# RWKV-7 attention with a hard-swish FFN on one core: FFN pieces moved ahead beside the second inversion, earlier K~ and B~, a denser third inversion

## Chip, cores and metric

One core of one Trainium2 chip. The metric is the device time of a whole execution in microseconds. Before and after are read from one profiled execution each, and the times from several executions of both on the same chip.

## The reference, cut to what matters

Two blocks follow each other. The attention runs a recurrence over 768 steps for 4 x 8 heads with a 40 x 40 state; its output, 3072 tokens of 320 features, goes through an FFN of width 2048.

```python
for t in range(S):
    y[:, :, t] = np.einsum('bhd,bhde->bhe', rt, state)
    Sa = np.einsum('bhde,bhe->bhd', state, at)
    state_decay = state * wt[:, :, None, :] - np.einsum('bhd,bhe->bhde', Sa, bt)
    state = state_decay + np.einsum('bhd,bhe->bhde', vt, kt)
...
h = x @ w_in
g = h * np.clip(h + 3.0, 0.0, 6.0) / 6.0
out = g @ w_out
```

## The kernel before

The sequence is cut into 24 units of work (`NK`; i below counts them from 0), four to a group (`NU`). A unit is prepared ahead of time (stages W, gam, A, B, K, F, factor, E, EV) and then stepped through (RT, R, C, S, U, UT, rS, sn, H, y, move). Each group needs one triangular inversion: a chain of about 60 short VectorE instructions that ends in the transposes tb (L552) and tt. RR (L625) is the product R plus EV, and S a turned copy of the state; U, UT and rS need them. The FFN of finished units is cut into pieces, nine for each half unit, that are handed out between attention stages to keep TensorE busy. `pieces(n)` hands out n pieces, `aside(n)` n steps of the inversion. The engines run their instructions in the order in which these calls are made, and that order is all the change touches.

One half unit of FFN (five pieces of expand, four of contract; each line with `yield` ends a piece):

```python
for c in range(2):
    for t in range(2):
        for i in range(NQ):
            nc.tensor.matmul(out=hp[c][:, i, :], lhsT=win[...], rhs=xt[:, t, :], ...)     # L806
        yield True
for i in range(NQ): ...
        nc.tensor.matmul(out=hp[c][:, i, :], lhsT=win2[...], rhs=xt[half(c), 2, :], ...)  # L811
for c in range(2):
    nc.scalar.activation(out=gt[:], in_=hp[c][:], func=AF.Relu, bias=three[:], scale=1.0) # L816
    nc.vector.scalar_tensor_tensor(out=gt[:], in0=gt[:], scalar=6.0, in1=hp[c][:], ...)   # L817
yield True
# contract, one half unit later:
            nc.tensor.matmul(out=op[:], lhsT=gts[c][:, n, :], rhs=wout[...], ...)         # L830
```

The inversion, and the product that needs its tb (L572):

```python
def invert(F, third):
    nc.vector.transpose(out=fb...)                                   # L531
    nc.gpsimd.affine_select(out=x...)                                # L534
    ...
    for i in range(1, L - 1):
        nc.vector.tensor_tensor(out=pv, ...)                         # L543
        yield
        nc.vector.tensor_tensor(out=rest, in0=rest, in1=pv, ...)     # L549
        yield
    nc.vector.transpose(out=tb..., in_=x[:])                         # L552
    yield
    nc.vector.transpose(out=tt..., ...)                              # L556
    ...

def third_block(F, tb, tt, n):
    ...
            nc.tensor.matmul(out=zp[x]..., lhsT=F..., rhs=tb..., ...)        # L572
```

The stages that a block can be given, and the loop over blocks (m counts blocks, four to a unit). A block issues all its products, then all their evictions (the copies out of PSUM), and takes its PSUM banks from five; when they don't suffice, `together` evicts in between:

```python
AHEAD_STAGES = [["W", "gam"], ["A", "B"], ["F", "K"], ["E", "factor"], ["EV"]]
...
for i in range(NU, NK):
    for j in range(BLOCKS):
        rate, inversion = 3.5, 0
        if i + AHEAD >= NK + NU - 1:
            rate = 4.5
        if i == NU and j == 0:
            inversion = 3
        a_block(m)
        if side and i > NU or i % NU == NU - 1 and rate < 4:
            rate, inversion = 6.2, 2
        if i % NU < 2 and j < 2:
            feed(rate / 2, inversion)
            if i % NU == 0:
                aside(3 * L)          # the rest of the inversion
            block(i, j)               # L572, L584
            rate /= 2
        feed(rate, inversion)         # piece, steps, piece, steps, ...
        m += 1
```

`factor` makes K~ and B~ (L473) out of the loaded K and B, and then issues the loads of the next unit's B and K into the same buffers.

Of the kernel before, what the change touches and what calls it, by code (L numbers as in the profile page):

```python
# [29 lines left out]
def kernel(  # L30
# [43 lines left out]
    B, H, T, D = r.shape  # L74
# [3 lines left out]
    NU = 2 * NP  # L78
# [447 lines left out]
    def invert(F, third):  # L526



        fb = inv.tile([P, L, L], F32, name="fb")  # L530
        nc.vector.transpose(out=fb[:].rearrange("p t s -> p s t"),  # L531
                            in_=F[:, :, 0:L].rearrange("p h s -> p s h"))
        x = inv.tile([P, L, L], F32, name="x", tag="x", bufs=1)
        nc.gpsimd.affine_select(out=x[:], in_=fb[:], pattern=[[1, L], [-1, L]],  # L534
                                compare_op=ALU.is_gt, fill=0.0, base=0, channel_multiplier=0)
        nc.gpsimd.memset(_ap(x[:], 0, [[L + 1, L]]), 1.0)
        for _ in range(3):
            yield
        prod = inv.tile([P, NH, L], F32, name="prod", tag="tt")
        for i in range(1, L - 1):  # L540
            n = L - 1 - i
            pv = _ap(prod[:], 0, [[i, n], [1, i]])
            nc.vector.tensor_tensor(  # L543
                out=pv, in0=_ap(x[:], (i + 1) * L + i, [[L, n], [0, i]]),
                in1=_ap(x[:], i * L, [[0, n], [1, i]]), op=ALU.mult,
            )
            yield
            rest = x[:, i + 1:L, 0:i]
            nc.vector.tensor_tensor(out=rest, in0=rest, in1=pv, op=ALU.add)  # L549
            yield  # L550
        tb = inv.tile([P, NH, L], F32, name="tb", tag="fb")
        nc.vector.transpose(out=tb[:].rearrange("p h t -> p t h"), in_=x[:])  # L552
        yield

        tt = inv.tile([P, NH, L], F32, name="tt", tag="tt")
        nc.vector.transpose(out=tt[:].rearrange("p h j -> p j h"),  # L556
                            in_=x[:].rearrange("p r j -> p j r"))
        third.append((F, tb, tt))
        for z in range(0, P, BL):
            yield  # L560
            nc.scalar.activation(out=tinv[z:z + L, :, 0:L], in_=tb[z:z + L], func=AF.Copy)
            nc.gpsimd.tensor_copy(tinv[z + L:z + BL, :, L:BL], tb[z + L:z + BL])
        yield
# [299 lines left out]
    def pieces(n):  # L863

        owed[0] += n
        while owed[0] >= 1:
            owed[0] -= 1
            if not next(stream):
                owed[0] = 0.0

    def aside(n, weight=0):

        for _ in range(n):
            if side and next(side[0], side) is side:
                side.popleft()
            for _ in range(weight):
                next(weights, None)
# [10 lines left out]
    third, F, group_F = [], None, []  # L888

    def prepared(i):  # L890
        nonlocal F
        if i >= NK:
            return None
        if i % NU == 0:
            F = inv.tile([P, NH, BL], F32, name="F", tag="F", bufs=2)
            group_F.append(F)
        return prepare(i, F)
# [39 lines left out]
    def block(i, j):  # L937

        if i % NU < 2:
            if j == 0:  # L940
                n = i % NU
                blocks[i] = third_block(*third[-1], 2 * n)
            run(blocks[i])
# [31 lines left out]
        pass  # L975
    for _ in range(16):
        aside(2)
        pieces(0.75)



    OWN_STAGES = [["RT", "VT"], ["R", "C", "S"], ["U", "UT", "rS"], ["sn", "H"], ["y"],
                  ["move", "move2"]]
    AHEAD_STAGES = [["W", "gam"], ["A", "B"], ["F", "K"], ["E", "factor"], ["EV"]]


    PRODUCTS = ["RT", "VT", "W", "S", "A", "B", "K", "factor",
# [5 lines left out]
    BLOCKS = 4  # L993

    def together(stages):

        begun, banks = [], 0

        def finish():
            begun.sort(key=lambda x: RESULTS.index(x[0]))  # L1000
            for _, rest in begun:
                for _ in rest:
                    pass
            begun.clear()
            shared[0] = None

        for name in PRODUCTS:
            for stage in stages.get(name, []):
                if name in TURNS:
                    need = 1  # L1010
                else:
                    width = WIDTH.get(name, NPR * BL)
                    need = 2 * (shared[0] is None or shared[1] + width > 512)
                if banks + need > 5:
                    finish()
                    banks, need = 0, 1 if name in TURNS else 2
                banks += need
                rest = stage()
                next(rest)
                begun.append((name, rest))  # L1020
        begun.extend((name, stage()) for name in stages if name not in PRODUCTS
                     for stage in stages[name])
        finish()

    begins = {u: max(3 * (u - 2 * NU), BLOCKS * (u - NU - AHEAD)) for u in range(2 * NU, NK)}
    coming, ahead, own = deque(range(2 * NU, NK)), {}, {}

    def a_block(m):

        if coming and begins[coming[0]] == m:  # L1030
            u = coming.popleft()
            ahead[u, m] = prepared(u), AHEAD_STAGES
        if m % BLOCKS == 0 and m // BLOCKS + NU < NK:
            i = m // BLOCKS + NU
            own[i, m] = step(i), OWN_STAGES
        stages = {}
        for (u, begin), (fs, order) in sorted(own.items()) + sorted(ahead.items()):
            if m - begin < len(order):
                for name in order[m - begin]:
                    stages.setdefault(name, []).append(fs[name])  # L1040
        together(stages)
        if any(u % NU == NU - 1 and m - begin == 2 for u, begin in ahead):
            third.clear()
            side.append(invert(group_F[-1], third))

    def feed(n, inversion):

        whole = int(n)
        for k in range(whole):
            pieces(1)  # L1050
            aside(inversion)
        pieces(n - whole)

    m = 0
    for i in range(NU, NK):
        for j in range(BLOCKS):
            rate, inversion = 3.5, 0
            if i + AHEAD >= NK + NU - 1:
                rate = 4.5
            if i == NU and j == 0:  # L1060
                inversion = 3
            a_block(m)
            if side and i > NU or i % NU == NU - 1 and rate < 4:
                rate, inversion = 6.2, 2
            if i % NU < 2 and j < 2:
                feed(rate / 2, inversion)
                if i % NU == 0:
                    aside(3 * L)
                block(i, j)
                rate /= 2  # L1070
            feed(rate, inversion)
            m += 1
    for _ in range(2):
        a_block(m)
        m += 1
# [32 lines left out]
```

## Time and profile before

| | before |
|---|---|
| time, median | 892.05 us (888.48 to 892.34, 4 runs) |
| span of the profiled execution | 891.7 us |
| TensorE busy | 791.5 us, 89% |
| TensorE idle from 195 to 406 us | 211 - 188.1 = 22.9 us |
| TensorE idle from 406 us to the end | 485.75 - 479.4 = 6.3 us, of it 4.3 behind its last product |

The last two rows tell where a change of order can gain: TensorE is full from the tenth unit (i = 9, at 406 us) on, so what counts is how early that point comes.

### The profile page before, as it was taken

The page shows a single profiled execution, that of the slowest core. Times are in us where ns is not written, and L with a number is a line of the kernel's source. Part 1 is how long each engine was busy: PE and PEld are TensorE (multiplying, and loading weights), DVE is VectorE, ACT ScalarE, POOL GpSimd, SP SyncE. Part 2 cuts the span into 40 slices and gives each one's busy share as a digit, 9 for nine tenths or more (in the row PEclk, how much of TensorE's full clock was granted, in tenths as well). Part 3 has the DMA queues.
Part 4 walks back from the last instruction along what each step waited for, and adds up shares of the span by engine and source line. Part 5 has one row for each costly group of instructions (what it writes and reads, how often), then busy time and mean ns, then how long its engine had stood idle before and what let it go on. Part 6 is the DMA issues. An engine that isn't in the chain of part 4 may idle for free.

```text
span 891.7 us, 36217 instructions
## 1 busy us (share of the span) xinstructions
PE 791.5 (89%) x16128; PEld 673.8 (76%) x16128; DVE 533.8 (60%) x1141; ACT 289.2 (32%) x694; POOL 152.1 (17%) x295
## 2 busy tenths in 40 slices
PE   4611878898698999899999999999999999999998
PEld 3511766777587787688888888888888888888886
DVE  7998777968744457835469744579544775122211
ACT  1334644232333222233323433322434233322211
POOL 4321010220121120211211311220222102000000
PEclk8755678998798899989999999999999999999999
DMA  6543333431122222203221222321232111010000
GB/s 131 89 113 93 111 107 93 73 69 20 34 41 56 36 45 47 46 20 63 52 41 37 47 48 42 58 43 36 49 56 42 25 26 23 17 25 17 19 18 15
DMA packets 175979, 45.08 MB, mean 51 GB/s; under 512 B 157904, under 2 KB 173264, under 8 KB 175824
## 3 DMA queue, kind: packets, MB, share of 16 engines
q1 hardware_dynamic: 174768, 42.61, 23.7%
q8 instruction: 127, 2.08, 1.0%
q10 hardware_dynamic: 1056, 0.16, 0.1%
q14 instruction: 28, 0.23, 0.1%
HBM read 34.08 MB, written 3.93 MB: 43 GB/s over the span
## 4 chain that ended last, share of the span: by engine, by line
PE 59%; issue 1%; DVE 1%; POOL 0%; DMA 0%; ACT 0%; SPq 0%
PE o L830 19%; PE h L806 16%; PE h L811 5%; PE any L358 4%; PE any L376 3%; PE any L708 2%; PE any L731 2%; PE any L653 1%; PE any L450 1%; PE any L572 1%; PE any L619 1%; PE any L584 1%; PE any L674 1%; PE any L690 1%; PE any L638 1%
## 5 line engine op out<-in xcount | busy, mean ns | idle before, releaser
L830 PE MATMUL o<-wout,gt 128*128 128x320 f32 x768 | 238.0, 455 | 0.2 <-DVE gt L817 0.2
L806 PE MATMUL h<-xt,win 128*128 128x128 f32 x1536 | 198.0, 283 | 0.6 <-issue 0.5
L806 PEld LDWEIGHTS h<-xt,win 128*128 128x128 f32 x1536 | 187.1, 196 | 10.5 <-issue 1.3
L830 PEld LDWEIGHTS o<-wout,gt 128*128 128x128 f32 x768 | 141.9, 194 | 56.8 <-issue 3.9
L817 DVE SCALAR_TENSOR_TENSOR gt<-gt,h 128x512 f32<-128x512 f32 x96 | 61.3, 680 | 93.2 <-ACT gt L816 93.2
L816 ACT ACTIVATE gt<-h,three 128x512 f32<-128x512 f32 x96 | 60.8, 686 | 136.1 <-PE h L811 136.1
L741 POOL TENSOR_TENSOR yg<-ys,gam 128x512 f32<-128x512 f32 x24 | 40.4, 1685 | 240.4 <-DVE ys L738 133.8
L543 DVE TENSOR_TENSOR prod<-x 128x30 f32<-128x30 f32 (+9 forms) x180 | 63.3, 352 | 11.7 <-POOL x L534 6.7
L549 DVE TENSOR_TENSOR x<-x,prod 128x30 f32<-128x30 f32 (+9 forms) x180 | 61.9, 344 | 4.4
L473 POOL TENSOR_TENSOR KBt<-K,rgt 128x320 f32<-128x320 f32 x24 | 23.9, 996 | 232.4 <-ACT rgt L465 214.0
L811 PE MATMUL h<-xt,win 64*128 64x128 f32 x768 | 55.8, 285 | 0.0
L385 DVE COPY_PREDICATED score<-mask,any 128x256 f32<-128x256 int32 x143 | 53.0, 431 | 0.0
L572 PE MATMUL any<-tb,F 32*32 32x32 f32 x768 | 16.6, 203 | 38.7 <-DVE tb L552 38.7
L715 DVE TENSOR_TENSOR state<-any,state 128x160 f32<-128x160 f32 x48 | 13.3, 316 | 62.9 <-PE any L376 58.4
L811 PEld LDWEIGHTS h<-xt,win 64*128 64x128 f32 x768 | 46.6, 187 | 5.1 <-issue 0.2
L412 DVE RECIPROCAL gam<-prods 128x256 f32<-128x256 f32 x24 | 41.4, 1738 | 14.1 <-POOL yg L741 14.0
L738 DVE TENSOR_TENSOR ys<-any,ys 128x256 f32<-128x256 f32 x48 | 18.1, 418 | 52.6 <-PE any L500 27.2
L572 PEld LDWEIGHTS any<-tb,F 32*32 32x32 f32 x768 | 15.3, 119 | 41.8 <-issue 40.9
L401 DVE TENSOR_TENSOR_SCAN prods<-wm,start 128x528 f32<-128x528 f32 x24 | 30.1, 1253 | 21.4 <-ACT wm L398 19.7
L427 DVE RECIPROCAL rgam<-prods 128x256 f32<-128x256 f32 x24 | 41.7, 1739 | 0.0
L625 DVE TENSOR_TENSOR RR<-any,EV 128x160 f32<-128x160 f32 x48 | 13.3, 317 | 43.6 <-PE any L376 38.5
L267 ACT ACTIVATE parts<-parts,low 128x256 uint32<-128x256 uint32 x40 | 20.3, 508 | 57.3 <-DVE parts L265 57.1
(136 smaller groups left out, 1177.5 us busy)
## 6 DMA issues: line engine op xcount, KB each, us to landing
raw<-in_moe_w_out_dram SPq DMA_DIRECT2D x20, 256.0 KB
B<-in_b_dram SPq DMA_DIRECT2D x48, 80.0 KB
K<-in_k_dram SPq DMA_DIRECT2D x48, 80.0 KB
V<-in_v_dram SPq DMA_DIRECT2D x96, 40.0 KB
R<-in_r_dram SPq DMA_DIRECT2D x96, 40.0 KB
out_dram<-ob SPq DMA_DIRECT2D x48, 80.0 KB
W<-in_w_dram SPq DMA_DIRECT2D x40, 80.0 KB
A<-in_a_dram SPq DMA_DIRECT2D x40, 80.0 KB
```

The lines of the kernel that those rows point to most:

```text
L385: nc.vector.copy_predicated(out=x[:, 4 * i:4 * i + 4, :], mask=mask4, data=o[i])
L412: nc.vector.reciprocal(gv[:, :, 0:HB], o["prods"][:, :, 0, 1:HB + 1][:, :, ::-1])
L427: nc.vector.reciprocal(rv[:, :, HB:BL], o["prods"][:, :, 1, 1:HB + 1])
L543: nc.vector.tensor_tensor(out=pv, in0=_ap(x[:], (i + 1) * L + i, [[L, n], [0, i]]), in1=_ap(x[:], i * L, [[0, n], [1, i]]), op=ALU.mult,)
L549: nc.vector.tensor_tensor(out=rest, in0=rest, in1=pv, op=ALU.add)
L572: nc.tensor.matmul(out=zp[x][z:z + L, h, :], lhsT=F[z + L:z + BL, n * H + h, L:BL], rhs=tb[z + L:z + BL, n * H + h, :], start=True, stop=True,
L741: nc.gpsimd.tensor_tensor(out=yg[:], in0=m["ys"][:].rearrange("p r q t -> p r (q t)"), in1=o["G"][:], op=ALU.mult)
L806: nc.tensor.matmul(out=hp[c][:, i, :], lhsT=win[:, t, j * P:(j + 1) * P], rhs=xt[:, t, :], start=(t == 0 and i == 0), stop=False)
L811: nc.tensor.matmul(out=hp[c][:, i, :], lhsT=win2[half(c), (j0 + i) * P:(j0 + i + 1) * P], rhs=xt[half(c), 2, :], start=False, stop=(i == N ...
L816: nc.scalar.activation(out=gt[:], in_=hp[c][:], func=AF.Relu, bias=three[:], scale=1.0)
L817: nc.vector.scalar_tensor_tensor(out=gt[:], in0=gt[:], scalar=6.0, in1=hp[c][:], op0=ALU.min, op1=ALU.mult)
L830: nc.tensor.matmul(out=op[:], lhsT=gts[c][:, n, :], rhs=wout[:, c * HJ + r * NQ + n, :], start=((split or r == 0) and c == 0 and n == 0), ...
```

## The change

The intent: fill the time in which TensorE waits for the second inversion with more FFN pieces and take them back behind it, get B earlier, and finish the third inversion before it is waited for. The whole diff:

```diff
     for _ in range(16):
         aside(2)
-        pieces(0.75)
+        pieces(1.25)
...
+    CLOSE_STAGES = [["W", "gam"], ["A", "B"], ["F", "K", "factor"], ["E"], ["EV"]]
...
             u = coming.popleft()
-            ahead[u, m] = prepared(u), AHEAD_STAGES
+            close = coming and begins[coming[0]] < m + BLOCKS
+            ahead[u, m] = prepared(u), CLOSE_STAGES if close else AHEAD_STAGES
...
+            if i < 2 * NU - 1:
+                rate = 3
             if i == NU and j == 0:
                 inversion = 3
             a_block(m)
             if side and i > NU or i % NU == NU - 1 and rate < 4:
-                rate, inversion = 6.2, 2
+                rate, inversion = 6.2, 2 + (i < 2 * NU)
```

I number the parts as the prediction does: 1 is 1.25 pieces, 2 is rate 3, 3 is CLOSE_STAGES, 4 is the third step per piece.

## The prediction

> **What bounds the kernel now.** I read the page first: TensorE is busy 89% of the span, VectorE 60%, the DMA engines a fifth.
>
> ```profile
> PE 791.5 (89%) x16128; PEld 673.8 (76%) x16128; DVE 533.8 (60%) x1141; ACT 289.2 (32%) x694; POOL 152.1 (17%) x295
> ...
> PE   4611878898698999899999999999999999999998
> ...
> PEclk8755678998798899989999999999999999999999
> ```
>
> A slice is 22.3 us. From slice 18 on, about 400 us, TensorE is full at full clock, so nothing there can be won except by doing less work, and the change removes none: the order of instructions shows 432 FFN pieces in both kernels. What can be won is idle time and slow-clock time of TensorE before 400 us. The change touches nothing before 220 us. So I listed the idle time of TensorE between 196 and 390 us, in the view of waits:
>
> ```profile
> PE any L572 <- DVE tb L552: 12.5, 2, 8.3
> PE any L358 <- DMA B<-in_b_dram: 3.4, 2, 2.9
> PE any L500 <- issue: 2.4, 1, 2.4
> PE any L500 <- DVE score L385: 1.7, 1, 1.7
> PE any L450 <- issue: 1.4, 2, 1.0
> PE any L376 <- DVE RR L625: 1.2, 1, 1.2
> ```
>
> The columns are total us, times, longest. The two L500 rows lie before 206 us and stay. The others are the goals of the change, and the timeline of TensorE places them:
>
> ```profile
> 232.89 1.92 PE L572 MATMUL any<-tb,F 32*32 32x32 f32 x64 [8.31 <-DVE tb L552]
> ...
> 285.86 1.09 PE L358 MATMUL any<-ident,B 128*128 128x128 f32 x4 [2.89 <-DMA B<-in_b_dram]
> ...
> 290.50 4.63 PE L830 MATMUL o<-wout,gt 128*128 128x320 f32 x8
> ...
> 341.72 1.09 PE L376 MATMUL any<-RT,VT 40*64 40x64 f32 x32 [1.16 <-DVE RR L625]
> ...
> 378.76 2.00 PE L572 MATMUL any<-tb,F 32*32 32x32 f32 x64 [4.20 <-DVE tb L552]
> ```
>
> After each gap the same products take about twice as long for a while: L830 x8 takes 4.63 us at 290.50 and 2.42 us when warm (at 280.10). Adding up the excess of the rows behind each gap over their warm twins: gap at the second inversion (8.31) 2.1 us; gap on B (2.89) 4.4 us; gap on RR (1.16) 2.1 us; gap at the third inversion (4.20) 2.4 us. Small gaps without a slow phase: 0.98, 0.26, 0.50, 0.44. Sum after 220 us: 18.7 idle and 11.0 slow clock, 29.7 us. This is all the change can win: 3.3% of 892.
>
> **What the Trainium skill says.** "TensorE: Matmul & The Clock Gate", Part 1 (the HAM clock gate), has the clock at half rate after an idle window of some 3.4 us and full again after as long a busy one. The trace agrees on the factor (4.63 against 2.42) but not on the limit: gaps of 2.89 and 1.16 us were enough. The same page, under "Architectural detail", calls ScalarE and VectorE strict first-in first-out. The trace agrees: at 216.84 VectorE waits 2.24 us for one FFN instruction while inversion steps that need nothing stand behind it. This row decides my first part. "PSUM — Partial Sum Buffer", Specifications, gives 8 banks; the kernel uses them as 5 + 2 + 1, so a block that needs a sixth bank of the five waits for an eviction. The waits in the built program agree.
>
> **Part 1, more pieces beside the second inversion (16 x 0.75 becomes 16 x 1.25).** By the order, 7 more pieces stand before the L572 that waits (51 against 44): L806 x24, L811 x16, L830 x16 more, less one L806 group moved behind. By the warm rows (L806 x32 3.65, L811 x16 1.1, L830 x16 4.4) the nine pieces of a group take 9.15 us; ten before L572 take 10.05 (with an L806 x8 of 0.9), three take 2.8 now (222.63 and 220.43), so 7.1 to 7.25 us of work more, and the gap is 8.31 us: it seems to fit. But what does VectorE do meanwhile?
>
> ```profile
> 216.84 1.28 DVE L817 SCALAR_TENSOR_TENSOR gt<-gt,h 128x512 f32<-128x512 f32 x2 [2.24 <-ACT gt L816]
> ...
> 224.09 1.25 DVE L401 TENSOR_TENSOR_SCAN prods<-wm,start 128x528 f32<-128x528 f32 x1
> 225.38 1.75 DVE L412 RECIPROCAL gam<-prods 128x256 f32<-128x256 f32 x1
> ...
> 230.84 1.91 DVE L552 STREAM_TRANSPOSE tb<-x 128x1024 f32<-128x1024 f32 x1
> ```
>
> The order of VectorE in the changed kernel has the first L817 pair six steps earlier, before an L549 that ran at 211.98, a second L817 pair behind 14 more steps, and then, as before, L610, scan L401, reciprocal L412, 13 inversion steps, L552. Follow it, with TensorE unchanged up to 220.43:
> - The first L817 cannot start before 216.84 (its h is done at 216.02). VectorE now idles from 211.95 instead of from 214.6: 4.9 us instead of 2.2.
> - L817 to 218.1; 14 steps of 0.435 to 224.2. The second L817 needs L811, which TensorE reaches after L806 x32 (3.65) and ends at 225.1; with ScalarE 225.95. L817 to 227.2; 6 steps to 229.6; L610 to 230.1.
> - The scan needs W turned. TensorE does L830 x16 until 229.5, then R, V, W until 230.8; the two ScalarE copies end at 231.8. Scan to 233.1, reciprocal to 234.8, 13 steps (3.8, from the rows 227.05 to 230.84) to 238.6, L552 to 240.5.
> So L572 starts at 240.5 instead of 232.9, 7.6 us later, while TensorE is through with its work at 231.7 (now 224.6). The gap is 8.8 us, not 1. The pieces don't fill the gap, they push it along, since VectorE waits for TensorE twice in the same stretch. Part 1 costs 7.6 - 7.1 = 0.5 us. The slow phase stays.
>
> **Part 2, rate 3 instead of 3.5 in the 12 blocks behind.** The pieces come back to the same count: by the order 128 pieces have been issued at the R of the tenth unit in both kernels, and all behind it is the same but for a piece or two. So any gain is the shift of that point, 405.95 us now. Each block has half a piece, 0.5 us, less cover. I followed the waits of the blocks: the tightest (masks of E for EV, two blocks with a scan) still hold within about 0.3 us. Cost 0 to 1, taken as 0.3.
>
> **Part 3, factor with K and F.** K~ and B~ free the buffers of B and K a block earlier, and the loads of B go out about 8 us sooner. Now B is issued at 282.47 and landed by 285.86, 3.4 us; 8 us is enough. The 2.89 us gap goes, with its 4.4 us of slow clock, and the 0.50 us at 311.82: -7.8 us. It costs a bank: in the first such block K, factor, U/UT and rS need six, and the program now waits in rS (L690) for the UT eviction, which at 277.48 to 279.30 came about 1.3 us behind its product. +1.3 us, and perhaps a slow phase: +0.8. In the later blocks the sixth bank comes from an early eviction and costs nothing.
>
> **Part 4, third inversion with 3 steps per piece.** L552 now comes two blocks earlier, so the 4.20 us gap and its 2.4 us go: -6.6. But steps are now denser than TensorE's cover. A block (number m=12 of the loop, at 327 us now) puts 18 steps and an L817 pair on VectorE behind its own results: those end at about 334.75 (no K~/B~ of POOL before yg any more, so a little sooner than now), then 3 steps, L817 1.2, 15 steps of 0.435: 343.5. Behind them stands RR (L625), now at 341.35. TensorE is through with the block's pieces at 336.4 and with S, A, B, EV, R at 338.8, then waits for RR until 343.9: 5.1 us instead of 1.16, +3.9; slow phase 2.7 (mean of the four) instead of 2.1, +0.6. Net of part 4: -2.1 us. I found no further gap in the next three blocks.
>
> **Sum.** +0.5 +0.3 -7.8 +2.1 -2.1 = -7.0. 892.3 - 7.0 = 885.3 us.
>
> **Rivals.**
> 1. The change does what its words say: the gaps at both inversions and on B all go, -2.1 -8.3 -7.8 -6.6 and no new one: about -27 with the small ones, 865 to 867. For it: the amount of work moved equals the gap. Against it: the two waits of VectorE above. It would need VectorE to run ahead of TensorE in 211 to 232 us, and the trace shows it waiting there already.
> 2. The denser inversion is worse than I think: RR late by more, a long slow phase, and a second gap in the block after: +6 on my sum, 891. For it: VectorE has 18 steps (6.3 us at their mean of 0.35), an L817 share of 0.9 and some 3.5 us of results in a block, 10.7 us, where a block lasts about 9.5. Against: only 66 steps are there, so it ends after four blocks.
> 3. Less cover in the 12 blocks opens a gap of about 0.5 in each: +6, 891. Against: two blocks measured now (297 to 327 us) have 0.94 us of idle altogether.
> 4. The load of B is late for another cause (the queue of SyncE, where an issue takes 0.65 us): then part 3 yields only half, 889. Against: the queue is seldom waiting on itself; it waited for L462 13.9 us.
>
> **Range and chances.** The sure part is B; the inversions are near zero with an error of about 4 us each way, mostly from how long the clock stays low, which the four gaps show as 2.1 to 4.4. Rivals 2 to 4 lie at 889 to 891, rival 1 in part at 875 to 880. Range 879 to 889.5. Faster by over 2% (under 874.4) needs most of rival 1: 5%. Slower by over 2%: 1%.
>
> **What would show it.** Right: the L572 of the second inversion still waiting 8 to 10 us for tb, now near 240.5; no wait on B; a wait for RR of 4 to 7 us near 340; that of the third without a wait; a wait of about 1.3 us in L690 near 256; R of the tenth unit near 399 instead of 405.95; everything behind it alike. Wrong: the L572 of the second inversion waiting under 3 us (then VectorE was not held by L817 and the scan), or no wait for RR (then the steps fit beside the pieces).

## The result and the profile after

| | before | after |
|---|---|---|
| time, median | 892.05 us | 884.41 us (883.57 to 885.67, 4 runs) |
| span of the profiled execution | 891.7 us | 882.8 us |
| TensorE busy | 791.5 us | 786.3 us |
| R of the tenth unit | 405.95 us | 396.85 us |

The ratio is 0.9925 (95%: 0.9897 to 0.9953). A ratio here is the mean time of one kernel's runs over that of the other's of the same rounds, so not quite the ratio of the medians quoted. It is a gain clear of noise, of 0.75%. TensorE is busy 5 us less with the same 16128 products: that is slow clock saved.

What does TensorE wait for now, from 196 to 390 us? The view of waits of the kernel after (total us, times, longest), against the same view of before in the prediction:

```profile
PE any L572 <- DVE tb L552: 8.5, 1, 8.5
PE any L376 <- DVE RR L625: 3.6, 1, 3.6
...
PE any L376 <- ACT S L643: 1.7, 1, 1.7
PE any L690 <- ACT UT L681: 0.8, 1, 0.8
PE any L674 <- DVE at L429: 0.7, 1, 0.7
```

The wait on B and one of the two on tb are gone; the wait for RR has grown and been joined by three small ones. Their places in the timeline of TensorE (start, us, product, and in brackets the idle time before it):

```profile
242.30 1.92 PE L572 MATMUL any<-tb,F 32*32 32x32 f32 x64 [8.54 <-DVE tb L552]
244.14 3.17 PE L806 MATMUL h<-xt,win 128*128 128x128 f32 x16
...
257.18 0.69 PE L690 MATMUL any<-RT,S 40*64 40x64 f32 x30 [0.77 <-ACT UT L681]
...
289.15 0.60 PE L358 MATMUL any<-ident,B 128*128 128x128 f32 x4
...
310.41 0.62 PE L674 MATMUL any<-tinv,RR 64*64 64x64 f32 x26 [0.74 <-DVE at L429]
...
337.96 0.32 PE L376 MATMUL any<-RT,VT 40*64 40x64 f32 x2 [1.69 <-ACT S L643]
341.84 1.13 PE L376 MATMUL any<-RT,VT 40*64 40x64 f32 x30 [3.56 <-DVE RR L625]
342.90 5.06 PE L806 MATMUL h<-xt,win 128*128 128x128 f32 x32
...
373.82 1.20 PE L572 MATMUL any<-tb,F 32*32 32x32 f32 x64
```

And VectorE's side of the two waits that stayed, in its timeline:

```profile
218.63 1.28 DVE L817 SCALAR_TENSOR_TENSOR gt<-gt,h 128x512 f32<-128x512 f32 x2 [5.52 <-ACT gt L816]
...
227.80 1.29 DVE L817 SCALAR_TENSOR_TENSOR gt<-gt,h 128x512 f32<-128x512 f32 x2 [1.91 <-ACT gt L816]
...
233.59 1.26 DVE L401 TENSOR_TENSOR_SCAN prods<-wm,start 128x528 f32<-128x528 f32 x1 [1.88 <-ACT wm L398]
...
240.34 1.90 DVE L552 STREAM_TRANSPOSE tb<-x 128x1024 f32<-128x1024 f32 x1
...
341.47 0.55 DVE L625 TENSOR_TENSOR RR<-any,EV 128x160 f32<-128x160 f32 x2
```

This execution ran 1.8 us behind the other before anything that the change touches: L811 stood at 214.92 before and stands at 216.72. Taken off, L572 comes at 240.5. VectorE waits three times in the 25 us before L552, 5.5 + 1.9 + 1.9 us, where before it waited once, 2.2 us; TensorE waits for VectorE at the end of it as long as before. The pieces have moved the gap and not filled it.

From the tenth unit on the two are alike. One line of the view of windows for each, from its R to its end (start:end and length, then busy us of each engine, granted clock of TensorE, where 1.00 is full speed, DMA share and GB/s); before:

```profile
405.95:891.70 485.75, 479.44 (x9593) 407.80 (x9591) 245.56 (x504) 149.72 (x348) 75.18 (x131) 1.00 0.19 36
```

and after:

```profile
396.85:882.80 485.95, 479.54 (x9593) 408.05 (x9591) 245.84 (x504) 149.85 (x348) 75.17 (x131) 1.00 0.19 36
```

So the whole gain is the earlier start of the tenth unit, 9.1 us in this pair of executions. Run by run the gain is smaller, 6 to 7 us by the two ratios (0.9925 here, 0.9932 in the rounds of e12), since the profiled execution of before was one of its slower ones: it took 893.46 us.

### The profile page after: what moved, and what is told of

Its sections match the earlier page's. It is cut to its first block, busy times and chain, and to the rows that moved or that the text cites. A ratio compares the mean times of both kernels' runs of the same rounds, so it can differ in the third digit from the quotient of the medians.

```text
span 882.8 us, 36229 instructions
## 1 busy us (share of the span) xinstructions
PE 786.3 (89%) x16128; PEld 671.5 (76%) x16128; DVE 533.7 (60%) x1141; ACT 290.4 (33%) x694; POOL 152.7 (17%) x295
## 4 chain that ended last, share of the span: by engine, by line
PE 74%; DVE 4%; issue 1%; POOL 0%; ACT 0%; DMA 0%; SPq 0%; DVEq 0%
PE o L830 23%; PE h L806 19%; PE h L811 5%; PE any L358 5%; PE any L376 3%; PE any L708 2%; PE any L731 2%; PE any L450 2%; PE any L572 1%; PE any L584 1%; PE any L653 1%; PE any L619 1%; PE any L674 1%; PE any L690 1%; DVE x L549 1%
## 5 line engine op out<-in xcount | busy, mean ns | idle before, releaser
L830 PE MATMUL o<-wout,gt 128*128 128x320 f32 x768 | 233.3, 448 | 0.0
L806 PE MATMUL h<-xt,win 128*128 128x128 f32 x1536 | 197.6, 283 | 0.5 <-issue 0.5
L806 PEld LDWEIGHTS h<-xt,win 128*128 128x128 f32 x1536 | 186.4, 196 | 9.4 <-issue 0.7
L830 PEld LDWEIGHTS o<-wout,gt 128*128 128x128 f32 x768 | 140.0, 192 | 55.4 <-issue 1.8
L817 DVE SCALAR_TENSOR_TENSOR gt<-gt,h 128x512 f32<-128x512 f32 x96 | 61.4, 681 | 103.4 <-ACT gt L816 103.4
L811 PE MATMUL h<-xt,win 64*128 64x128 f32 x768 | 55.8, 285 | 0.0
L811 PEld LDWEIGHTS h<-xt,win 64*128 64x128 f32 x768 | 46.6, 187 | 5.0 <-issue 0.2
L572 PE MATMUL any<-tb,F 32*32 32x32 f32 x768 | 16.6, 203 | 34.8 <-DVE tb L552 34.8
L572 PEld LDWEIGHTS any<-tb,F 32*32 32x32 f32 x768 | 15.2, 119 | 37.5 <-issue 28.1
L605 ACT ACTIVATE RT<-any 128x512 f32<-128x512 f32 x24 | 14.3, 596 | 75.1 <-PE any L358 75.0
```

Source lines behind the costliest of these rows:

```text
L806: nc.tensor.matmul(out=hp[c][:, i, :], lhsT=win[:, t, j * P:(j + 1) * P], rhs=xt[:, t, :], start=(t == 0 and i == 0), stop=False)
L811: nc.tensor.matmul(out=hp[c][:, i, :], lhsT=win2[half(c), (j0 + i) * P:(j0 + i + 1) * P], rhs=xt[half(c), 2, :], start=False, stop=(i == N ...
L830: nc.tensor.matmul(out=op[:], lhsT=gts[c][:, n, :], rhs=wout[:, c * HJ + r * NQ + n, :], start=((split or r == 0) and c == 0 and n == 0), ...
```

## The experiments

My theory: each wait stands on one order of instructions, VectorE serves its queue in order, and what the change gains is the wait on B. Rivals: each part does what its words say (rival 1 of the prediction), or one of them costs what another gains. Twelve kernels ran, in three calls of four, each call on one chip with its own runs of the kernel before. Each result was correct.

| run | what | median us | before us | ratio (95%) |
|---|---|---|---|---|
| e1_close | before + part 3 | 886.58 | 888.86 | 0.9966 (0.9940 to 0.9992) |
| e2_dense | before + part 4 | 887.69 | 888.86 | 0.9979 (0.9952 to 1.0006) |
| e3_pieces_rate | before + parts 1, 2 | 902.36 | 888.86 | 1.0138 (1.0087 to 1.0189) |
| e4_pieces | before + part 1 | 903.52 | 888.86 | 1.0147 (1.0100 to 1.0194) |
| e10_no_close | after - part 3 | 895.65 | 889.39 | 1.0061 (1.0029 to 1.0093) |
| e11_no_dense | after - part 4 | 892.92 | 889.39 | 1.0035 (0.9999 to 1.0071) |
| e12_after_again | after | 884.07 | 889.39 | 0.9932 (0.9901 to 0.9964) |
| e5_flush | after, inversion ahead of W | 879.43 | 889.98 | 0.9878 (0.9831 to 0.9926) |
| e6_rr | after, thin in m = 12 | 880.31 | 889.98 | 0.9885 (0.9858 to 0.9913) |
| e7_steps3 | after, 3 steps a round | 874.40 | 889.98 | 0.9818 (0.9788 to 0.9848) |
| e8_warm | after, gap filled | 881.31 | 889.98 | 0.9904 (0.9874 to 0.9934) |
| e9_both | e7 + e6 | 868.92 | 889.39 | 0.9761 (0.9730 to 0.9791) |

### The parts alone

**Part 3 alone.** Edit: only CLOSE_STAGES and its use.

> The kernel before with part 3 alone (factor with K and F for the close units). My account: the wait of 2.9 us on the load of B and its slow phase of 4.4 us go, a wait of about 0.8 to 1.3 us in L690 comes: 5.7 us less, about 886. The waits at both inversions (8.3 and 4.2 us) stay. Rival (B is late because of the queue of SyncE): half of the wait stays, about 889. Rival 1 (each part works as its words say) agrees with mine here.

Measured: 0.34% less, 3 us where I expected 5.7. 3 us is the figure of the rival (half of the wait on B stays), but its half wait is not there: the mechanism is as I expected. The waits of TensorE from 220 us on no longer name B:

```profile
PE any L572 <- DVE tb L552: 12.5, 2, 8.3
...
PE any L690 <- ACT UT L681: 0.8, 1, 0.8
```

The size is off. One reason that the traces show is that a gap's slow phase is not the same in each execution. Here a gap of 1.65 us ahead of RR's product has almost none, where one of 1.16 us in the kernel before made L830 x8 take 4.11 us:

```profile
334.08 0.92 PE L376 MATMUL any<-RT,VT 40*64 40x64 f32 x32 [1.65 <-DVE RR L625]
334.93 2.42 PE L830 MATMUL o<-wout,gt 128*128 128x320 f32 x8
```

And in e2, which keeps the gap on B, that gap is 1.99 us with about 1.6 us of slow clock, not 2.89 with 4.4. In the profiled execution of e1, which was the fastest of the four, the way from the fifth unit's R to the tenth's is 174.3 us instead of 184.6 with the same pieces: 10 us, where the runs have 3. A pair of traces does not measure a gain of this size; which gap accounts for the missing 2.7 us is not shown.

**Part 4 alone.**

```diff
-                rate, inversion = 6.2, 2
+                rate, inversion = 6.2, 2 + (i < 2 * NU)
```

> The kernel before with part 4 alone (3 steps per piece beside the third inversion). My account: the L572 of the third inversion no longer waits (4.2 us and 2.4 us of slow clock less), but the L376 behind RR waits 5 us instead of 1.2, with 2 to 3 us of slow clock: about 2 us less in all, 890. Rival 1: both waits go, 6.6 to 9.9 us less, 883 to 885. Rival 2: a second gap follows, 4 us more, 896.

Measured: 0.21% less, 1.9 us; my account said 2. The interval reaches past 1 (0.9952 to 1.0006), so the time alone shows no gain; the waits show the account. The L572 of the third inversion doesn't wait, and RR takes its place, with the 1.7 us for S ahead of it:

```profile
343.24 1.13 PE L376 MATMUL any<-RT,VT 40*64 40x64 f32 x30 [2.90 <-DVE RR L625]
```

**Parts 1 and 2 alone, and part 1 alone.**

```diff
-        pieces(0.75)
+        pieces(1.25)
...
+            if i < 2 * NU - 1:
+                rate = 3
```

(the last two lines in the first of the runs only)

> The kernel before with parts 1 and 2 (1.25 pieces beside the second inversion, rate 3 behind it). My account: L572 of the second inversion starts 7 to 8 us later and still waits 8 to 9 us; no gain, 0 to 1 us more than before. Rival 1: that wait goes to under 2 us and its slow phase with it, 8 to 10 us less, about 883. Rival 3 (less cover opens gaps in the 12 blocks): 4 to 6 us more, 897.

> The kernel before with part 1 alone (rate stays 3.5). My account: the same wait of 8 to 9 us at L572, time as before within 1 us; against the run with parts 1 and 2 it shows what the lower rate costs: 0 to 0.5 us. Rival 1: 8 to 10 us less than before. A third view: without the lower rate the FFN runs ahead of its inputs and pieces are skipped later, so it is 3 us or more slower than parts 1 and 2 together.

Measured: both 1.4 to 1.5% slower, some 12 to 13 us. The wait at the second inversion is as I expected, 8.55 and 7.67 us, and rival 1 is out. But the time is not: I expected no change. In part 1 alone, a wait that no other kernel here has so often stands second (from 220 us to the end):

```profile
PE any L572 <- DVE tb L552: 11.7, 2, 7.7
PE h L806 <- DMA xt<-yg: 9.2, 7, 2.4
```

The FFN has caught up with its input x, which attention makes unit by unit. Counting pieces in the order of instructions up to the R of the tenth unit gives 134 with part 1, 130 with parts 1 and 2, 128 before and after. In part 1 alone the way from there to the end takes 494.1 us with 6 pieces fewer to do than before, which needs 485.75: all of the loss, and more, lies there. The third view in my expectation had the reason: the FFN is ahead of its input, and pieces are skipped. The ninth unit has 15 pieces in this trace where before has 17, and in the order of the program three calls find no x ready and hand out nothing, in the blocks 17, 33 and 50. Its size was wrong: the lower rate makes up for only 1 us (1.0147 against 1.0138), which the noise covers. With parts 1 and 2 the loss lies earlier: waits on B of 2.4 and 3.4 us, twice the total of before (6.7 against 3.4 us), and 2.4 us on x at 403 us.

### What the parts are worth inside the change

These two runs were made because the parts alone don't add up: 3 and 1.9 us less and 12.3 us more make 7.4 us more, and the change has 6 to 7 us less.

**Without part 3** (AHEAD_STAGES for all units):

> The changed kernel without part 3. The FFN count at the tenth unit stays 128 here. If the lower rate of part 2 (shorter blocks) is what makes B late, then three waits on B of 2.4, 3.4 and 0.6 us with their slow phases stand here as with parts 1 and 2 alone, and the time is 8 to 12 us over the changed kernel, 893 to 896; so part 3 is worth more inside the change than the 3 us it is worth alone. If the parts add, 3 us over it, 887.

Measured: 11.4 us over the changed kernel in the same rounds. The waits on B stand as expected:

```profile
291.72 0.63 PE L358 MATMUL any<-ident,B 128*128 128x128 f32 x4 [2.49 <-DMA B<-in_b_dram]
...
315.45 0.63 PE L358 MATMUL any<-ident,B 128*128 128x128 f32 x4 [3.30 <-DMA B<-in_b_dram]
```

They are 7.3 us in all four places, with a granted clock of 0.95 and 0.90 in the two units around them where the changed kernel has 1.00. The lower rate of part 2 makes the blocks shorter, B is needed sooner behind its issue (waits on B of 2.6 us in all with part 1 alone, 6.7 with parts 1 and 2), and part 3 is what pays for that. Issue and use tell the same: before, B was issued at 282.47 and used at 285.86; after, at 278.87 and at 289.15.

**Without part 4:**

> The changed kernel without part 4. The third inversion then lasts into the block m=16, which keeps the rate of 6.2 there: the FFN count at the tenth unit is 130 instead of 128. If that is what made parts 1 and 2 alone wait for x at 403, 530 and 655 us, such waits of 2.4, 0.8 and 1.5 us stand here too. L572 of the third inversion waits 4.5 us again, RR 1 us. By the sum of my terms 2 us over the changed kernel, 886; with the waits for x 4 to 8 us over it, 890.

Measured: 9.1 us over the changed kernel. From its timeline:

```profile
376.20 2.01 PE L572 MATMUL any<-tb,F 32*32 32x32 f32 x64 [4.56 <-DVE tb L552]
...
391.47 1.13 PE L806 MATMUL h<-xt,win 128*128 128x128 f32 x8 [1.16 <-DMA xt<-yg]
```

An inversion that is still going in block 16 keeps the rate of 6.2 there, so 16 pieces instead of 14 are handed out in the ninth unit, and x is waited for again (at 391, 517 and 642 us, 2.8 us in all, as in e3 at 403, 530 and 655; a fourth wait of 0.9 us, at 286, lies before block 16 and stands in e6 and e8 too, which have part 4). The ninth unit takes 39.5 us instead of 28.0, of which 2 are those pieces; the eighth is 3.7 us shorter than in e12, since R's sum RR is waited for 2.17 us and not 5.27 with S. This leaves some 6 us of the 9. The profiled executions of e11 and e12 differ by only 7.0 us, so some of the rest is spread between executions; I did not settle it further.

### Is VectorE's order what holds tb?

**The rest of the inversion ahead of the block with W:**

```diff
+            while m == 0 and not third:
+                aside(1)
             a_block(m)
```

> The changed kernel, with the rest of the second inversion (13 steps and both transposes) put ahead of the block with the W scan, so that VectorE no longer waits for W, scans and takes the reciprocal before L552. If those hold tb: L552 ends near 237 instead of 242.2, the wait at L572 falls from 8.5 to about 3.3 us, 5 us less than the changed kernel, about 879. If tb is held by the length of the inversion alone, the wait stays over 7 us and the time does not change.

Measured: ratio 0.9878, 4 to 5 us less than the changed kernel (0.9925 in its first rounds, 0.9932 in those of e12). The runs spread more than others, 876 to 884 us, and the interval (0.9831 to 0.9926) just reaches the change's ratio; the wait shows the effect better:

```profile
236.04 1.92 PE L572 MATMUL any<-tb,F 32*32 32x32 f32 x64 [3.40 <-DVE tb L552]
```

3.40 us against 3.3 expected: scan, reciprocal and the wait for W were on the path. The length of the inversion alone does not hold tb.

**More steps in each round:**

```diff
     for _ in range(16):
-        aside(2)
+        aside(3)
         pieces(1.25)
```

> The changed kernel with 3 inversion steps ahead of each 1.25 pieces instead of 2, in the 16 rounds beside the second inversion. In my account both sides then fit: VectorE waits 2.8 us instead of 5.5 for the first L817, the rest of the inversion runs ahead of the scan, L552 ends near 233, TensorE comes to L572 near 233.6 and does not wait: 8.5 us and 1.8 us of slow clock less than the changed kernel, about 874. If the gap only moves again, the time does not change by over 2 us.

Measured: 874.4 us, about 10 us under the changed kernel. VectorE and TensorE in it:

```profile
219.53 1.28 DVE L817 SCALAR_TENSOR_TENSOR gt<-gt,h 128x512 f32<-128x512 f32 x2 [2.25 <-ACT gt L816]
...
231.44 1.98 DVE L552 STREAM_TRANSPOSE tb<-x 128x1024 f32<-128x1024 f32 x1
```

```profile
234.58 1.20 PE L572 MATMUL any<-tb,F 32*32 32x32 f32 x64
235.71 2.05 PE L806 MATMUL h<-xt,win 128*128 128x128 f32 x16
```

L552 now stands ahead of the scan and is done before TensorE gets there. This is rival 1's picture, reached: the same pieces fill the gap once the steps are dense enough to be VectorE's work in that time. What the change lacked was not pieces but steps. Whether 3 steps with the old 0.75 pieces would do as well was not tried.

### Is RR held by the steps ahead of it?

```diff
-                rate, inversion = 6.2, 2 + (i < 2 * NU)
+                rate, inversion = 6.2, 2 + (i < 2 * NU) - 2 * (m == 12)
```

> The changed kernel with 1 step per piece instead of 3 in the one block m=12 of the third inversion. If RR stands behind 18 steps in VectorE's order: RR comes near 336.6 instead of 341.5, the wait for RR of 3.6 us goes (that for the copy S of 1.7 us stays), its slow phase of 1.8 us shrinks: 4 to 5 us less than the changed kernel, about 880, and the third L572 still does not wait. If the wait for RR has another cause (bank, S), it stays and the time does not change.

Measured: ratio 0.9885, about 4 us under the changed kernel.

```profile
340.08 0.33 PE L376 MATMUL any<-RT,VT 40*64 40x64 f32 x2 [1.07 <-DVE RR L625]
...
341.20 3.84 PE L806 MATMUL h<-xt,win 128*128 128x128 f32 x32
```

5.25 us of waits have become 1.24 (the 1.7 us put down to S, which I expected to stay, are gone too), the L806 x32 behind them takes 3.84 us instead of 5.06, and no later gap appears.

### The slow clock by itself

72 transposes of the identity that nothing needs, written ahead of L572 into the bank that it overwrites (lines of this kernel are 9 higher: L581 is L572). Wasted work on purpose; the result stays right.

```diff
+            for _ in range(WARM):          # 72
+                nc.tensor.transpose(out=_ap(zp[0][:], 0, [[1, P]]), in_=ident[:],
+                                    identity=ident[:])
```

> The changed kernel with 72 idle transposes (7.9 us at 0.11 us each) into the bank of the second inversion's product ahead of L572: they fill the gap with work that nothing needs, to measure the slow clock by itself. If the slow phase follows from the gap: L572 x64 takes 1.2 us instead of 1.9 and L806 x16 2.05 instead of 3.2, 1.8 us less than the changed kernel, about 882.6, with the gap filled. If the slow phase does not follow from the gap, the durations stay.

Measured: ratio 0.9904, 2 to 2.5 us under the changed kernel, for work that does nothing. The change's ratio lies within this run's interval (0.9874 to 0.9934); the durations are what shows the effect:

```profile
237.01 1.20 PE L581 MATMUL any<-tb,F 32*32 32x32 f32 x64 [0.75 <-DVE tb L552]
238.14 2.05 PE L815 MATMUL h<-xt,win 128*128 128x128 f32 x16
```

1.92 and 3.17 us have become 1.20 and 2.05. So the slow phase follows from the idle gap, and this gap's costs 1.8 us, beside its own 8.5.

### Both remedies

> The changed kernel with both remedies: 3 steps per round beside the second inversion, and 1 step per piece in the block m=12 of the third. If the two waits are separate, their gains add: about 10 us (measured alone) and about 4 us less than the changed kernel, 869 to 872, ratio to before 0.975 to 0.98. If the second gain is taken back later, it stays at that of the first remedy alone, 0.982.

Measured: 868.92 us, ratio 0.9761, 2.4% faster than before and 1.7% faster than the change. The gains add. The profile of this kernel can't be used: that execution alone fell into a slow state, 1284.28 us at a granted clock of 0.558, and the five others took 867.86 to 871.27 at 0.935 to 0.940.

> The changed kernel itself, to be compared in the same rounds with the ones of this call: about 884, ratio 0.992 to 0.994.

884.07 us, 0.9932: the result of the change repeats.

## Why the prediction was right, point by point

885.3 us predicted, 884.41 measured; the forecast of a gain of under 2% held.

- **Gap at the second inversion.** 8.8 us predicted, near 240.5; 8.54 us measured, at 240.5 once the early 1.8 us are taken off. Right, by the steps given: the first L817 waits (4.9 predicted, 5.5), the second (1.75 in my working, 1.9), the scan for W (1.7, 1.9). e5 shows it for the scan and the wait for W, e7 for the order as a whole.
- **Slow phase behind it.** 2.1 predicted, 1.8 measured, shown by e8.
- **B.** The wait went, with that at 311.82: B is issued 10.3 us ahead of its use instead of 3.4. Its slow phase was mis-sized: 4.4 us was what one execution had, and e1 gained 3 us in all where the sum had 5.7.
- **L690.** 1.3 us predicted, 0.77 measured, without the 0.8 of slow clock. The claim that later blocks with a sixth bank cost nothing was wrong by 0.74 us: L674 at 310.41 waits for the eviction of A.
- **RR.** 5.1 us predicted; 1.69 + 3.56 = 5.25 measured, the first part on S, which I had not separated. Slow phase 2.7 predicted; 0.46 + 1.33 = 1.8 measured (L376 1.13 and L806 5.06 against 0.67 and 3.73). e6 shows the cause.
- **Third L572, tenth unit, tail.** No wait, as predicted. 399 predicted, 396.85 measured. Tail alike within 0.2 us.
- **The parts as separate terms: wrong.** The sum gives part 1 +0.5 us and part 2 +0.3 us. Part 1 alone costs 13 us, parts 1 and 2 together 12. The step that failed is "the pieces come back to the same count": it credits part 2, but the count is 128 only with part 4, which ends the rate of 6.2 in block 16; without it 130 and x is waited for (with part 4 alone it is 125). And part 3 was priced by the waits on B of the kernel before, while with part 2's shorter blocks those waits would be 7.3 us: inside the change it is worth 11.4 us, not 5.7. The total came out near because the working followed the order of the whole changed program. The terms are not what an engineer would get by taking one part away. Parts 1 and 2 were not taken out of the change: what they are worth inside it, and whether parts 3 and 4 gain more without them, is not shown.
- **Luck in the total.** In the traced pair, the way from L811 (214.92 before, 216.72 after) to the tenth unit's R became 10.9 us shorter, where the sum has 7.0. The three small gaps that the sum left in place (0.98, 0.26 and 0.44 us) are gone, in e1 (part 3 alone) as well; L690 and RR cost less too. The runs have 6 to 7 us. That the total lies within 1 us of 884.41 is in part luck.

## What to carry to other kernels

Moving work into an idle gap fills it only if the engine that ends the gap isn't waiting for the engine that gets the work. Look at that engine's queue first: an instruction that needs the moved work, ahead of the one waited for, carries the gap along. Parts of a schedule that share a budget (pieces handed out, lead of a load) have to be tested by taking each out of the whole as well as alone, and a rate belongs with the count of what it has handed out by a fixed point.

## What the Trainium skill lacked or had wrong

- "TensorE: Matmul & The Clock Gate", Part 1: an idle window of about 3.4 us as the limit. Here products behind gaps of 2.89 and 1.16 us took twice their time (L830 x8 4.63 and 4.11 us against 2.42), while L358 right behind gaps of 2.49 and 3.30 us was not yet slow (0.63 us) and the products after the first of these were (L708 1.07 against 0.66). The page says that the window runs freely; a rule by the length of one gap doesn't follow from it, and in e1 L830 x8 took 2.42 us behind a gap of 1.65.
- The same page, Part 1, says that the clock gate has been seen stuck at a quarter of its speed for over 50 us. Here one execution of e9 ran at a mean granted clock of 0.558, with the digit 5 (in tenths of full speed) in all 40 slices of its page but the first, 1284.28 us against 868.9, and the next five did not.
- The same page, "Part 4: PE-mode transpose", says that transposes do not count as busy time for the clock gate in the same way. Here 72 of them in an 8.5 us gap, 8.02 us in all, kept the clock up: the products behind them took 1.20 and 2.05 us instead of 1.92 and 3.17, and the kernel's time fell by 2 to 2.5 us, within the noise. That idle gaps are worth filling with idle work is on no page.
- No page says that ordered queues carry a gap along when work is moved into it; the runs show 8.31 us before and 8.54 us after 7 us of work were moved.
